# A gated recurrence followed by a highway layer: three pieces of work change engine and the order list is replaced

## The chip, the cores and the metric

The kernel runs on one core of a Trainium2 chip, in one launch. The metric is device microseconds (us) of the whole execution. The core's engines are named as the profile names them: PE (TensorE), with PEld for its weight loads; DVE (VectorE); ACT (ScalarE); POOL (GpSimd); SP, which here only starts DMAs. Each engine works through its own instructions strictly in their order, and waits on semaphores for the others.

## What is computed

```python
B, S, D = 4, 6336, 256
f = lower_bound + (1 - lower_bound) * sigmoid(f_logit)      # B x S x D
h = f[:, t] * h + (1 - f[:, t]) * x[:, t]                   # for every t: y[:, t] = h
y = y.reshape(B * S, D)                                     # 25344 tokens
H = maximum(y @ w_h, 0);  T = sigmoid(y @ w_t + b_t)
out = T * H + (1 - T) * y                                   # float32
```

Inputs are float32: `x` and `f_logit` of 26 MB each, two 256x256 weight matrices, and two vectors. The output has 26 MB.

## The kernel before

The tokens are cut into 25 units: 24 of 1024 tokens of one batch (8 blocks of 128 tokens), and a last one of 8 blocks of 96 tokens that holds the rest of all four batches. A unit goes through a *front* (load, gate, transpose, scan) and a *back* (highway layer, store). At the beginning units are cut finer: unit 0 has fronts 0, 1, 2 of 2, 2 and 4 blocks, units 1 and 2 have two fronts of 4 blocks (3, 4 and 5, 6), and from front 7 on a front is a whole unit. The last unit has fronts 28 and 29 and backs 24 and 25, of 4 blocks. There are 30 fronts and 26 backs; back j uses the scan of front j+4, for j of 3 and more.

Each step has a letter, and the program is written by a list of letters, `PLAN` (L349). The next letter X takes the next piece of kind X. What an engine does, and in which order, is fixed by this list alone. A digit behind A, B, Z, G or O names the PSUM slot that the step writes: slots 0 and 1 for the transposes A and B, slots 0, 1 and 2 for Z, G and O. A slot can be written again when its reader is done. The letters, with the engine and the line:

- L, X (SP, L106): load `f_logit` or `x` of a front, from five buffers each; Q (SP, L125): load one of the two weight matrices. R (SP, L309): store half a back.
- U (ACT, L154): u = sigmoid(-f_logit) for a front. A (PE, L198): transpose u. F (ACT, L205): the decay f, from PSUM.
- P (POOL, L160) and p (DVE, L166): the product bv = u * x of two blocks; a whole unit has four. B (PE, L215): transpose bv. S (DVE, L230): the scan, one for each half of the 256 channels; it reads f and B's PSUM slot.
- W (DVE, L148): scale the weights of one half of the channels; two in all, ahead of the first G.
- G, Z (PE, L245): the two matrix products of a back, four matmuls for each half of the channels. D (DVE, L256): relu with the scaled y, from G's slot. T (ACT, L251): sigmoid, from Z's slot.
- E (DVE, L166) and H (POOL, L160): e = d * t. In a full back, E does the first 512 columns and H the other 512 (`SHARE`).
- O (PE, L296 and L297): the sum with y, transposed back, for half a back. C (ACT, L303) and V (DVE, L303): copy it out of PSUM; V has a share in the last three backs only.

`F4.1` below is the second step F of front 4, `C2.0` the first copy of back 2; steps without a number are all of their kind for that front. DVE's products (E and p) go through `vector_mul`, POOL's (P and H) through `gpsimd_mul`, and the next POOL product in the list after a DVE product is made to wait for it:

```python
def gpsimd_mul(out_, a, b):
    ins = pin(nc.gpsimd.tensor_mul(out_, a, b))
    while port:
        tc.add_manual_dep(ins.ins, port.pop().ins.name, ...reason="shared port")
```

Of the kernel before, what the change touches and what calls it, by code (L numbers as in the profile page):

```python
# [19 lines left out]
def kernel(  # L20
# [19 lines left out]
    P = 128  # L40
    NH = D // P
    NB = 8
# [16 lines left out]
    fronts, backs = [], []  # L59
# [6 lines left out]

    LASTQ = 2

    EARLY = [(0, 0), (2, 0)]

# [40 lines left out]
    def shape(piece):  # L113

        u, j0, j1 = piece
        return units[u][0], j1 - j0
# [34 lines left out]
    def gate(i):  # L151
        np_, nb = shape(fronts[i])
        u = fs[i]["u"] = new("u", [NB, D], FP16)
        pin(nc.scalar.activation(u[:np_, :nb], fs[i]["lt"][:np_, :nb], AF.Sigmoid, scale=-1.0))  # L154
# [13 lines left out]
    def product(i, k, mul):  # L168
        np_, _ = shape(fronts[i])
        if "bv" not in fs[i]:  # L170
            fs[i]["bv"] = new("bv", [NB // 2, D, 2], BF16)
        mul(inner(fs[i]["bv"][:np_, k:k + 1])[:, 0], fs[i]["u"][:np_, 2 * k:2 * k + 2],
            fs[i]["xt"][:np_, 2 * k:2 * k + 2])

    def width(piece):
        np_, nb = shape(piece)
        return np_ * nb
# [81 lines left out]
    SHARE = 512  # L259

    def shared(j):

        return SHARE if width(backs[j]) == NB * P else 0

    def e_cols(j, a, e):
        if "e" not in bs[j]:
# [3 lines left out]
    def e_dve(j):  # L270
        vector_mul(*e_cols(j, 0, width(backs[j]) - shared(j)))

    def e_pool(j):
        gpsimd_mul(*e_cols(j, width(backs[j]) - shared(j), width(backs[j])))
# [37 lines left out]
    def each(pieces, count):  # L312
        return [(i, k) for i, piece in enumerate(pieces) for k in range(count(piece))]

    def halves_of(pieces):
        return each(pieces, lambda p: len(halves(p)))
# [22 lines left out]
        "D": (d_dve, each(backs, lambda p: NH)),  # L339
        "E": (lambda j, _: e_dve(j), each(backs, lambda p: 1)),  # L340
        "H": (lambda j, _: e_pool(j), [(j, 0) for j in range(len(backs)) if shared(j)]),
        "O": (o_pe, groups),
        "C": (lambda j, q: o_copy(j, q, nc.scalar.copy, 0, group(j, q)[2]), [p for p in groups if group(*p)[2]]),
# [3 lines left out]
    }  # L347

    PLAN = (  # L349
        "LLXXLXQQUUA0pFFB1PSLXLXLXLSA0B1UFFpSSWWA0PFFUXLXLB1PSA0PSUFFUPPG0G1Z2B1DDSZ0STTA0B1PPHEFFUPSXXLA0SPF"  # L350
        "FUO1B0O2LLXXA1PSSPCCFFUPG0G1B0PPPDSSDZ2Z0A1A0TTFFEZ2B1Z0A0TTUFG1G2SDDB1HPPPPHPO0O1B0UCCSSZ2A1G0Z1B0E"
        "DTFTPPSPPPA1O2G0O1DHFUCCB1A0G0Z2Z1SFTTA1B0DEPSLLLXXRXRRLXRRRFUPG2O0B1O1A0DPPHCCG2FSDZ0Z1A1B0G2EPSTTF"
        "UPO0O1B1DPPHCCA0G2Z0SFDZ1A1B0EPSTFTUPG2O0A1B0O1DPPHCCG2Z0FSDA0B1Z1EPRRRRXLLSTFTPO2G0B0O1DPUCCESZ0G2A"
        "1Z1TFDB0A1G0PHPSDTFUO2B1O1CCPPPHSA0G0Z2Z1B1DFTEPSA0G0O2TPFDPPHB0O1G0A1UCCFSXLRXRRLRRRLLRXXDZ2Z1B0A1E"
        "PSTTFPO0G2B1A0O1DPPHCUCFSG0Z2Z1B1A0DEPSTTFPG0O2B0O1A1DPPHUCFCSG0Z2DA1B0Z1EPSG0PTFTDPPHB1O2O1G0A0UCCS"
        "Z2B1Z1FTDEPXRXRRRLRSTPA0O0G2O1B1DPPHFCCSA0G0Z2Z1B1DUFTEPSA0G0O2TPFCO1B0A1G2DPPHCSFUDZ0Z1A1B0G2EPSTTF"
        "PLLRRXLXRRXRRDPPHO0O1B0A1CCSFUG0Z2Z1A1B0DTTFEPSPG0O2O1B0A1DPPHCCFUSZ2G0A1B0Z1DEPSTTFPG0O2O1B0A1DPPHC"
        "CFUSG2Z0B1Z1A0RLRRRRXLRXXLLDEPSTFTPG2O0B0O1A1DPPHCUCFSG2Z0B0Z1A1DTTFEPSG2O0B0O1A1PDPPHCUCFSG2Z0B0Z1A"
        "1TFTDEPSPG2O0B1A0G1UCFDPPHSDO2Z0B1A0Z1TFTCPSPG0B0A1EZ1O2FTCUDSG0A1Z1B0RRRRRXRREDHFFO2G0B1TCPSRO1A0O2"
        "PCCFDSERG0G1RDSHZ2Z0B1DFTTSZ2G1O0HTTSDDCO2G1EERDO0CDO2CVRO1RCVZ0RCVTRTEO2O1CVRR"  # L360
    )
    assert all(PLAN.count(k) == len(places) for k, (_, places) in kinds.items())
    todo = {k: iter(places) for k, (_, places) in kinds.items()}
# [31 lines left out]
```

## Time and profile before

| | |
|---|---|
| median of 8 runs | 215.13 us (214.9 to 215.7) |
| the profiled execution | 215.03 us, span 213.2 us |
| busy, share of the span | PE 88%, DVE 92%, ACT 91%, POOL 77% |
| DMA | 78.7 MB, 16 engines busy for 92.7% of the span on the SP queue |
| first scan starts, last copy ends | 8.32 us, 209.72 us |

The span runs from the first instruction to the last in the trace; 1.8 us of the execution's time lie outside it. Rows of groups read: line, engine, operation, output and inputs, shape, count, then busy us and mean ns of one, then the engine's idle time before them and who ended it. Rows of a timeline begin with the start and the duration in us. Instructions of one engine overlap a little in the trace, so that sums are made with the distance from one start to the next where a row gives it.

### The profile page before, as it was taken

To read this page: it belongs to the slowest core of one execution; us is meant where nothing else is said; L and a number is where in the kernel's file an instruction comes from. 1 tells how busy PE (TensorE), PEld (TensorE's weight loads), DVE (VectorE), ACT (ScalarE), POOL (GpSimd) and SP (SyncE) were. 2 spreads that over 40 slices of the span, in tenths; PEclk is the share of its full clock that TensorE was granted. 3 is DMA by queue.
4 is the path that set the end of the run, shared out by engine and by line. 5 is a ranking of instruction groups with operands and counts; after the bars stand their busy time and mean duration, and the time that the engine had idled before them with its cause. 6 is when DMAs were issued, how large, how long until landed. Compare 5 with 4: busy or idle time off the path is not lost.

```text
span 213.2 us, 4575 instructions
## 1 busy us (share of the span) xinstructions
PE 186.7 (88%) x1773; PEld 132.2 (62%) x1800; DVE 196.0 (92%) x156; ACT 194.3 (91%) x194; POOL 164.8 (77%) x134
## 2 busy tenths in 40 slices
PE   0477797889999999999999999999999999999861
PEld 0244764666866666776575777577667667676651
DVE  1599698999999999999999999999999999999971
ACT  4569979999999999999999999999999999996851
POOL 4269987989789988978988897898898889646500
PEclk9999699999999999999999999999999999999997
DMA  4999999999999999999999999999999998547085
GB/s 98 401 421 421 420 417 422 422 414 418 422 416 421 416 417 421 417 420 416 420 421 417 420 415 422 420 397 420 417 410 377 365 277 336 182 184 288 7 350 194
DMA packets 22725, 78.68 MB, mean 369 GB/s; under 512 B 2352, under 2 KB 2864, under 8 KB 22704
## 3 DMA queue, kind: packets, MB, share of 16 engines
q1 hardware_dynamic: 22160, 78.39, 92.7%
q8 instruction: 14, 0.23, 0.4%
q10 hardware_dynamic: 544, 0.00, 0.1%
q14 instruction: 7, 0.06, 0.1%
HBM read 52.43 MB, written 25.95 MB: 368 GB/s over the span
## 4 chain that ended last, share of the span: by engine, by line
PE 39%; ACT 27%; DMA 13%; DVE 12%; issue 5%; SPq 1%; ACTq 0%; DVEq 0%
DMA lt<-in_f_logit_dram 11%; PE gp L245 10%; PE zp L245 9%; ACT f L205 9%; ACT t L251 8%; ACT u L154 7%; DVE y L230 6%; PE op L296 6%; PE op L297 6%; DVE d L256 5%; PE uT L198 5%; PE bT L215 4%; ACT o L303 3%; DMA xt<-in_x_dram 2%; DVE e L166 1%
## 5 line engine op out<-in xcount | busy, mean ns | idle before, releaser
L160 POOL TENSOR_TENSOR bv<-u,xt 128x512 bf16<-128x512 f16 (+1 forms) x98 | 111.9, 1174 | 27.1 <-DVE e L166 9.6
L230 DVE TENSOR_TENSOR_SCAN y<-f,y,bT 128x1024 bf16<-128x1024 f16 (+3 forms) x56 | 106.6, 1917 | 0.8 <-ACT f L205 0.3
L205 ACT ACTIVATE f<-uT,ncc 128x1024 f16<-128x1024 f16 (+3 forms) x60 | 67.5, 1143 | 1.1 <-PE uT L198 1.1
L256 DVE SCALAR_TENSOR_TENSOR d<-y,ncc,gp 128x1024 bf16<-128x1024 bf16 (+1 forms) x52 | 62.5, 1208 | 0.9 <-PE gp L245 0.7
L251 ACT ACTIVATE t<-zp,bt 128x1024 bf16<-128x1024 f32 (+1 forms) x52 | 61.3, 1279 | 1.3 <-PE zp L245 0.9
L245 PEld LDWEIGHTS <-w_sb 128*128 128x128 f16 x400 | 37.8, 98 | 36.8 <-issue 5.0
L154 ACT ACTIVATE u<-lt 128x2048 f16<-128x2048 f32 (+3 forms) x30 | 54.0, 1800 | 6.0 <-DMA lt<-in_f_logit_dram 5.8
L303 ACT COPY o<-op 128x1024 f32<-128x1024 f32 (+2 forms) x50 | 54.2, 1188 | 5.2 <-PE op L297 5.2
L160 POOL TENSOR_TENSOR e<-d,t 128x1024 bf16<-128x1024 bf16 x24 | 51.6, 2150 | 8.7 <-DVE e L166 7.4
L297 PE MATMUL op<-ident_b,e 128*128 128x128 bf16 (+1 forms) x400 | 50.3, 221 | 2.9 <-DVE e L166 1.7
L296 PE MATMUL op<-diag,y 128*128 128x128 f16 (+1 forms) x400 | 50.4, 221 | 0.8 <-ACT t L251 0.7
L245 PE MATMUL gp<-y,w_sb 128*128 128x512 bf16 (+1 forms) x178 | 49.0, 382 | 1.8 <-DVE d L256 0.7
L245 PE MATMUL zp<-y,w_sb 128*128 128x512 bf16 (+1 forms) x195 | 49.1, 376 | 1.3 <-DVE y L230 0.8
L297 PEld LDWEIGHTS <-e 128*128 128x128 bf16 (+1 forms) x400 | 45.0, 115 | 7.1 <-DVE e L166 2.0
L296 PEld LDWEIGHTS <-y 128*128 128x128 bf16 (+1 forms) x400 | 45.1, 115 | 2.3
L215 PE MATMUL bT<-ident_f,bv 128*128 128x128 f32 (+1 forms) x200 | 32.3, 285 | 8.5 <-ACT f L205 2.6
L198 PE MATMUL uT<-ident_h,u 128*128 128x128 f16 (+1 forms) x400 | 31.7, 224 | 7.0 <-ACT u L154 5.4
L198 PEld LDWEIGHTS <-u 128*128 128x128 f16 (+1 forms) x400 | 26.9, 100 | 14.2 <-ACT u L154 5.8
L215 PEld LDWEIGHTS bT<-ident_f,bv 128*128 128x128 f32 (+1 forms) x200 | 23.0, 145 | 16.1 <-POOL bv L160 4.4
L166 DVE TENSOR_TENSOR e<-d,t 128x1024 bf16<-128x1024 bf16 (+1 forms) x26 | 18.5, 714 | 1.1 <-ACT t L251 1.0
L230 DVE TENSOR_TENSOR_SCAN y<-f,bT 128x512 bf16<-128x512 f16 (+2 forms) x8 | 10.5, 1342 | 3.1 <-PE bT L215 3.1
L303 DVE COPY o<-op 128x512 f32<-128x512 f32 (+1 forms) x4 | 2.8, 689 | 1.8 <-PE op L297 1.1
(20 smaller groups left out, 8.8 us busy)
## 6 DMA issues: line engine op xcount, KB each, us to landing
out_dram<-o SPq DMA_DIRECT2D x48, 512.0 KB, 13.5
lt<-in_f_logit_dram SPq DMA_DIRECT2D x21, 1024.0 KB, 15.0
xt<-in_x_dram SPq DMA_DIRECT2D x21, 1024.0 KB, 16.3
lt<-in_f_logit_dram SPq DMA_DIRECT2D x5, 512.0 KB, 7.9
xt<-in_x_dram SPq DMA_DIRECT2D x5, 512.0 KB, 8.6
xt<-in_x_dram SPq DMA_DIRECT2D x2, 384.0 KB, 10.6
lt<-in_f_logit_dram SPq DMA_DIRECT2D x2, 384.0 KB, 16.3
lt<-in_f_logit_dram SPq DMA_DIRECT2D x2, 256.0 KB, 4.0
```

The lines of the kernel that those rows point to most:

```text
L154: pin(nc.scalar.activation(u[:np_, :nb], fs[i]["lt"][:np_, :nb], AF.Sigmoid, scale=-1.0))
L160: ins = pin(nc.gpsimd.tensor_mul(out_, a, b))
L198: pin(nc.tensor.transpose(uT[:, j * np_:(j + 1) * np_], fs[i]["u"][:np_, j, h * P:(h + 1) * P], ident_h[:np_, :np_]))
L205: pin(nc.scalar.activation(f[:, :N].rearrange("p (k q j) -> p k q j", q=np_, j=j), fs[i]["uT", h].rearrange("p (k j q) -> p k q j", q=np_, ...
L215: pin(nc.tensor.transpose(t[:, k // r, k % r], fs[i]["bv"][:np_, k, h * P:(h + 1) * P].rearrange("p d j -> p (d j)").bitcast(FP32), ident_ ...
L230: pin(nc.vector.tensor_tensor_scan(y, fs[i]["f", h][:, c:c + w], fs[i]["bT", h][:, c:c + w], 0.0 if prev is None else prev, op0=ALU.mult, ...
L245: pin(nc.tensor.matmul(p[:, a:e], w_sb[:, k, ki, h * P:(h + 1) * P], y_of(j)[:, ki, a:e], start=ki == 0, stop=ki == NH - 1))
L251: pin(nc.scalar.activation(bs[j]["t"][:, m, :width(backs[j])], bs[j]["zp", m], AF.Sigmoid, bias=bt[:, m:m + 1]))
L256: pin(nc.vector.scalar_tensor_tensor(bs[j]["d"][:, m, :width(backs[j])], y_of(j)[:, m], ncc[:, m:m + 1], bs[j]["gp", m], op0=ALU.mult, op1 ...
L296: pin(nc.tensor.matmul(o, y[:, h, cols], diag[:, h], start=True, stop=False))
L297: pin(nc.tensor.matmul(o, bs[j]["e"][:, h, cols], ident_b, start=False, stop=True))
L303: pin(copy(bs[j]["o", q][:np_, a:e], bs[j]["op", q][:np_, a:e]))
```

## The change

Three things differ.

- `EARLY` is empty. The products of front 0 and the first one of front 2, which DVE made (p), are made by POOL (P).
- `shared` is 512 only from back 3 on. In backs 0, 1 and 2 one E of 1024 columns does all of e, and there is no H.
- `PLAN` is another list throughout, with 823 steps instead of 826.

The change is described as "GpSimd scales the weights instead of VectorE; VectorE alone computes e of the first three full backs; new list with measured durations". In the code W is the same in both kernels: `weights` (L147) issues on `nc.vector`, and the diff doesn't touch it. W's two steps stand at other places of the list.

```diff
-    EARLY = [(0, 0), (2, 0)]
+    EARLY = []
...
     def shared(j):
 
-        return SHARE if width(backs[j]) == NB * P else 0
+        return SHARE if width(backs[j]) == NB * P and j >= 3 else 0
...
     PLAN = (
-        "LLXXLXQQUUA0pFFB1PSLXLXLXLSA0B1UFFpSSWWA0PFFUXLXLB1PSA0PSUFFUPPG0G1Z2B1DDSZ0STTA0B1PPHEFFUPSXXLA0SPF"
-        "FUO1B0O2LLXXA1PSSPCCFFUPG0G1B0PPPDSSDZ2Z0A1A0TTFFEZ2B1Z0A0TTUFG1G2SDDB1HPPPPHPO0O1B0UCCSSZ2A1G0Z1B0E"
-        "DTFTPPSPPPA1O2G0O1DHFUCCB1A0G0Z2Z1SFTTA1B0DEPSLLLXXRXRRLXRRRFUPG2O0B1O1A0DPPHCCG2FSDZ0Z1A1B0G2EPSTTF"
-        "UPO0O1B1DPPHCCA0G2Z0SFDZ1A1B0EPSTFTUPG2O0A1B0O1DPPHCCG2Z0FSDA0B1Z1EPRRRRXLLSTFTPO2G0B0O1DPUCCESZ0G2A"
...
-        "1TFTDEPSPG2O0B1A0G1UCFDPPHSDO2Z0B1A0Z1TFTCPSPG0B0A1EZ1O2FTCUDSG0A1Z1B0RRRRRXRREDHFFO2G0B1TCPSRO1A0O2"
-        "PCCFDSERG0G1RDSHZ2Z0B1DFTTSZ2G1O0HTTSDDCO2G1EERDO0CDO2CVRO1RCVZ0RCVTRTEO2O1CVRR"
+        "XLLLXXLUUA0A1PFFFFUB0PSSA1B0FUFPSSPA0B1XQQLXLXLLXPPWFFUSSWB0A1PFUFPSSPXXLLXLG0Z1B0A1Z2PTFUFTPPG1B1DS"
+        "SDSSUEA0Z0G1G2A1DDPFTFFPPZ0B0A1O1O2PSSTFECCUB1B0Z0G1G2SDSDA1Z1TUFTPPPPPPA1G0B0FLXRLXRXLXLDESA1O1Z2Z0"
+        "UFCTTB1G1A0O2O0SDPPPFCCB0A1Z2G1O0FTUCB1G2PPHPPSDSEDPA0Z1Z0B1O2FTTUCESG1A0G0B1DDHPPPPSO2Z1O0UFTCCB0SA"
...
+        "UFCDEXXLRRRLLXXRRRRRLB1A0Z2G1PSTTFO0DCB1A0Z2G1O0PPHSFUCTDEB0A1G1Z0O2PPSDFTCB1A0G0SFPPHDO1A0B1Z2G0EUC"
+        "TFPPSO1PZ2CDTB0A1Z1G0SFTUHO2A1B0DFG1EPPPPSO0A1CCZ2DFB0Z0O1B1TTCUSESHPPG2A0Z0G1DDRRRRRRRRFFTB0A1O0Z2Z"
+        "1FCFSEHTTG0B1G2O1RSDDCO0SRHCZ2G1STRO0TDDEZ2CTERTG1O0O2DVDCO0CVEVRO1CRO2RCVRR"
     )
```

What moves in the list, in steps:

- The loads begin X0 L0 L1 L2 X1 X2 L3 X3, then Q Q, then L4. Before, they began L0 L1 X0 X1 L2 X2, then Q Q, then L3.
- DVE begins S0 S1 W S2 W S3 D0.0 S4 D0.1 S5 E0 D1.0 D1.1 S6 E1. Before: p S0 p S1 W W S2 D0.0 D0.1 S3 E0 S4 S5 D1.0 S6 D1.1 E1, where E was half as wide.
- PE has the O steps of back 0 behind A7.1, and before had them behind A5.
- At the end, after the last scan, PE has O22.1 Z25 G25 O23.0 O23.1 O24 O25. Before it had O22.1 G25 O23.0 O23.1 O24 Z25 O25.

## The prediction

> **What bounds the kernel now.** I read the page's busy line, then the engines' busy time by stretch, then VectorE's timeline at both ends. These are the stretches; after the stretch and its length come the busy us of PE, PEld, DVE, ACT and POOL, the granted clock, the DMA share and GB/s:
>
> ```profile
> 0.00:20.00 20.00, 10.53 (x59) 6.54 (x60) 12.41 (x20) 12.32 (x18) 10.59 (x20) 1.00 0.88 329
> 20.00:40.00 20.00, 15.94 (x139) 11.60 (x142) 16.85 (x14) 18.62 (x20) 17.21 (x14) 0.91 1.03 420
> 40.00:60.00 20.00, 18.39 (x181) 13.09 (x182) 20.00 (x13) 20.00 (x19) 18.30 (x15) 1.00 1.02 417
> 60.00:120.00 60.00, 57.03 (x564) 40.92 (x571) 59.78 (x41) 60.00 (x56) 53.01 (x41) 1.00 1.03 419
> 120.00:180.00 60.00, 58.34 (x565) 41.19 (x572) 59.51 (x41) 60.00 (x57) 52.57 (x40) 1.00 1.02 392
> 180.00:200.00 20.00, 19.63 (x181) 13.08 (x183) 20.00 (x20) 17.84 (x22) 11.90 (x9) 1.00 0.50 190
> 200.00:213.20 13.20, 6.81 (x100) 5.83 (x98) 7.41 (x13) 5.52 (x9) 1.25 (x1) 0.90 0.59 220
> ```
>
> From 40 to 180 us ACT is never idle, DVE idles 0.7 us and PE 6 of 140 us. There is nothing to gain there and something to lose. DVE idles 10.7 us before 40 us and 5.8 after 200; ACT idles 9.1 and, from 180 on, 9.8. So a change pays in two places: how early both engines have their first work behind them, and how tightly the last backs drain. DMA is full until near 180 us and half idle at the end: loads matter in the first 45 us.
>
> VectorE's timeline at both ends (start, duration, instruction, idle before it and who ended it):
>
> ```profile
> 6.74 0.73 DVE L166 TENSOR_TENSOR bv<-u,xt 128x512 bf16<-128x512 f16 x1 [1.33 <-DMA xt<-in_x_dram]
> 9.91 0.73 DVE L166 TENSOR_TENSOR bv<-u,xt 128x512 bf16<-128x512 f16 x1 [0.33 <-DMA xt<-in_x_dram]
> 26.24 2.33 DVE L230 TENSOR_TENSOR_SCAN y<-f,bT 128x512 bf16<-128x512 f16 x2 [1.84 <-PE bT L215]
> 34.02 1.40 DVE L166 TENSOR_TENSOR e<-d,t 128x1024 bf16<-128x1024 bf16 x1 [0.50 <-ACT t L251]
> ...
> 201.90 1.15 DVE L166 TENSOR_TENSOR e<-d,t 128x1024 bf16<-128x1024 bf16 x2
> 207.34 0.56 DVE L166 TENSOR_TENSOR e<-d,t 128x768 bf16<-128x768 bf16 x1 [0.48 <-ACT t L251]
> 209.03 0.69 DVE L303 COPY o<-op 96x512 f32<-96x512 f32 x1 [1.13 <-PE op L297]
> ```
>
> The 1.84 us at 26.24 is S5: on PE, its transposes B5 stood behind O0.0, and O0.0 waited 1.2 us for H0, which POOL made from 21.04 on in 2.60 us. In the new list O0 stands behind A7.1 and there is no H0. The tail's two waits are one chain: T25 is late, so E25, O25 and the last copy are.
>
> **The engine moves.** Prices by shape:
>
> ```profile
> L160 POOL TENSOR_TENSOR bv<-u,xt 128x512 bf16<-128x512 f16 x94 | 107.3, 1175 | 27.1 <-DVE e L166 9.6 <-DVE bv L166 6.6 <-DMA xt<-in_x_dram 3.8
> L160 POOL TENSOR_TENSOR e<-d,t 128x1024 bf16<-128x1024 bf16 x24 | 51.6, 2150 | 8.7 <-DVE e L166 7.4 <-ACT t L251 1.3
> L166 DVE TENSOR_TENSOR e<-d,t 128x1024 bf16<-128x1024 bf16 x24 | 17.5, 728 | 0.6 <-ACT t L251 0.5
> ```
>
> DVE loses two products of 0.73 us. It made E0, E1, E2 in 0.67, 1.40 and 1.12 us; a full-width E has no row. Two halves in a row took 1.15 us (201.90), twice the row stretched beside POOL would be 2.8; I take 1.2, the nearer row, because in the new list the next POOL step waits for each of these E and none runs beside it. Sum: 3 x 1.2 - 3.19 - 1.46 = -1.05 us of DVE work. POOL: 2 x 1.175 - 3 x 2.15 = -4.1 us, off the path, since it idles some 36 us. The added wait is P7.0 behind E0 (until 28.15 in the walk below). P7.1 to P7.3 queue behind it, until 32.8; B7 waits for them and is done at 33.5. S7.0 has E1 in front of it on DVE until 34.15, so E1 hides the wait by 0.65 us; a later E0 beyond that would delay S7 one for one. "GpSimd scales the weights" isn't in the code; W costs DVE its 2 x 0.70 us as before.
>
> On the price of moving a product to POOL, the row says 1.175 against 0.73 us, a factor of 1.6. The Trainium skill (GPSIMD Engine Reference, 4.1 Engine selection) advises against it: two-input elementwise work is about twice as slow there. By its factor a moved product would cost 1.46 us, 0.3 us more on the way to the first scan.
>
> **The ramp, walked.** Waits that ended on a load date them: L0 4.15, L1 5.84, X0 6.74 for the first three 256 KB; then 1536 KB by 8.53 and 5632 KB by 18.80 us, or 399 KB per us. In the new order X0, L0, L1 take those three times, L2 (1280 KB) 7.9, L3 11.0, the weights (3584 KB) 13.7, before 11.1, and L4 15.0, as before. So U0 starts at 5.84, not 4.15. P0 follows on POOL until 7.7; B0 ends at 8.8 and S0 starts at 8.85 (before 8.32). B1 stands behind A2, which needs U2 (ends 9.9): S1 11.15 (10.53). W0.0 at 13.7, S2 14.4 (13.23), W0.1, S3 17.45 (18.76, because two D stood before it). The A4 step needs S2's slot and starts at 16.85. G0 17.55, D0.0 19.8, S4 21.0, D0.1, S5 24.55 (26.24), E0 26.9, D1 28.15, S6 30.55, E1 32.9, S7.0 34.15 (35.87). From 14.4 on DVE has no idle time in this walk: its input is ready each time, by 0.1 to 3 us. It reaches the same finished work (S9.1, E3, D4.1) at 56.7, where it was 58.00: 1.3 us earlier. ACT, with U8 at 32.95 (L8 lands at 31.7), finishes the same set (F10.0, T4.1, C2.1) at 55.0 instead of 55.84: 0.85 us earlier. ACT is the engine that is never idle afterwards, so the ramp is worth -0.85. Bounds: -1.3 (DVE's lead) to +1.0 (one more wait such as the 1.84 at 26.24).
>
> PE's clock in the ramp: in 20 to 40 us it was 0.91, since 0.107 us lay between O0's matmuls instead of 0.055 from 23.70 to 26.2, after a PE wait of 1.2 us. A second such spell would cost 1.25 us, inside the upper bound above. The Trainium skill (TensorE: Matmul & The Clock Gate, Part 1) has the clock halve only after an idle window of about 3.4 us; no PE gap of the walk is that long, so by the page nothing is charged, while the row shows a shorter gap ahead of one.
>
> **The middle.** Per unit the work is the same. Steps there are U 1.80, F 1.0 x 2, T 1.0 x 2, C 0.9 x 2 on ACT, 7.6 us, and S 2.26 x 2, D 1.18 x 2, E 0.60 on DVE, 7.5. In the new list around units 24 and 25, F24.1 may start 0.65 us earlier to 1.0 us later than steady before either ACT or the scan waits: the PSUM slots leave some slack but not much. I charge the new order 0.65 us, as much idle time again as DVE showed between 40 and 180; bounds 0 and 2.
>
> **The tail.** Measured from S27.0 (186.36 before), DVE has the same work until the last scan, 14.6 us on (200.95). Before, Z25 stood behind O23 and O24 on PE, so T25 ran at 206.26, E25 at 207.34, the last copy 209.03 to 209.72: 23.4 us after S27.0. In the new list Z25 follows the last scan: Z25 0.85, C22.1, T25 until 17.0, D25.0, O23.0 until 17.4, V23.0, D25.1, V23.1 until 19.3, E25 19.85, O25.1 until 20.6, V25.1 20.7 to 21.4. That is -1.95 us, and DVE's idle time after 201.9 (0.29 + 0.20 + 0.20 + 0.48 + 1.13 = 2.3) is the most it can give. F28 comes up to 1.6 us later here (T21.1 stands behind F27.1), covered by S27.1; without that cover it would be 1.6 us back. I take -1.9, bounds -2.3 and 0. From the last copy to the end stay 3.5 us, the last store.
>
> Sum: -0.85 + 0.65 - 1.9 = -2.1, from the profiled 215.03 to 212.9 us. The median of all runs, 215.13, is 0.1 above that execution; 0.2% of this time, 0.43 us, is about what its measurement can tell from no change.
>
> **The rivals.** First, the middle takes the lead back: ACT and DVE are full there for 140 us, and a lead of 1 us only shifts where each waits, while the tail gives half (-0.95). With a charge of 0.9 to 2 in the middle that is 215.03 - 0.85 - 0.95 plus the charge, 214.1 to 215.2; 214.7 at 1.5. For it: DVE's E recurred every 7.46 us at 54 to 76 and 7.62 at 167 to 175, so the faster engine already waits for the other. Against it: the tail's reorder doesn't depend on that.
>
> Second, slower than before: the new list makes ACT wait once in each unit, for a PE step queued behind a slot that isn't free (O18.1 stands ahead of A26 and B25.1, for instance). Place: the 18 units between 45 and 180 us. ACT showed waits of 0.35 (181.44) and 0.58 us (192.82) of this kind when units were no longer regular. At 0.25 us a unit it is 4.5 us against the 2.75 gained, 216.8; it decides from 0.15 us a unit on. For it: PE is 95 to 97% busy there and takes steps in strict order. Against it: the slack above.
>
> Third, more than forecast: no charge in the middle, and DVE's whole lead counts, -1.3 - 1.95: 211.8.
>
> **How the numbers follow.** The forecast has 0.48, the first rival 0.16, the slower one 0.22, the third 0.14. The first lies half within 0.43 us of 215.03. Faster by over 0.2%: 0.48 + 0.14 + 0.08 = 0.70, less 0.03 for the forecast's own upper end: 0.67. Same: 0.08 + 0.02 = 0.10. Slower 0.23. The range goes from 211.0 (the sum of the lower bounds, -3.6, gives 211.4; the runs spread by 0.8 us, so 0.4 to a side) to 216.6, which leaves out over half of the slower rival (0.12) and a few in 100 at the low end. The forecast's own range is 211.4 to 214.8: all terms at their lower bounds, or one of them at its upper.
>
> **What would show it.** Right: S0 near 8.9, W0.0 near 13.7, no DVE idle of over 0.3 us between 15 and 57; D4.1 ends near 56.7; E after 201 without the two waits on T25 and O25, the last copy about 21.5 us after S27.0. Wrong: ACT idle between 60 and 180 us; PE's clock below 0.9 for more than one spell; weights that land after 15 us, which holds S2, A4, F4 and U5 behind W0.0 one for one.

## The result and the profile after

The changed kernel takes 216.29 us (median of 11 runs, 215.5 to 217.05), the old one 215.13 beside it (32 runs). The ratio is 1.005, with an interval of 1.0037 to 1.0063: slower by half a per cent, where 1% faster was forecast. Its profiled execution took 215.5 us with a span of 213.6. It is the fastest of its runs; two more profiles of the same kernel, below, are nearer to the median and show what this one hides.

The stretches of that execution (stretch, its length, busy us of PE, PEld, DVE, ACT and POOL, granted clock, DMA share, GB/s):

```profile
0.00:20.00 20.00, 8.45 (x48) 5.55 (x49) 9.17 (x16) 10.80 (x17) 12.66 (x20) 1.00 0.87 328
20.00:40.00 20.00, 17.32 (x135) 10.77 (x137) 19.71 (x16) 19.43 (x20) 12.50 (x11) 1.00 1.02 420
...
60.00:120.00 60.00, 57.91 (x573) 41.18 (x578) 59.27 (x40) 60.00 (x56) 53.85 (x42) 1.00 1.03 419
120.00:180.00 60.00, 58.43 (x560) 40.68 (x566) 59.87 (x41) 60.00 (x57) 51.07 (x40) 1.00 1.02 399
...
200.00:213.60 13.60, 6.82 (x91) 5.56 (x88) 7.17 (x13) 5.20 (x10) 1.16 (x1) 0.94 0.67 252
```

In the middle ACT is still never idle, so the slower rival of the prediction (a wait of ACT in every unit) did not come. DVE is busy for 3.2 us less in the first 20 us: two products have left it, and its steps D come later. The granted clock of 1.00 in the first row misleads: the trace has no record of the clock before its first change, at 20.9 us, and the matmuls' own durations show half speed until then.

Both sums of the prediction can be read as distances between the same steps. From the start of S9.0 to that of S27.0: 135.8 us before, 136.2 after, +0.4 (forecast +0.65). From S27.0 to the end of the last copy: 23.36 before, 22.21 after, -1.15 (forecast -1.95). From there to the end of the span: 3.5 before, 5.1 after, 5.0 in the two other profiles (forecast: no change). And S9.0 started at 50.53 before, and at 50.11, 51.41 and 51.02 in the three profiles of after: from 0.4 ahead to 0.9 behind, where 0.85 to 1.3 ahead was forecast. So the tail lost 0.3 to 0.5 us instead of giving 1.9, the middle took a little less than was charged, and the ramp went from a gain to a loss in two of the three profiles.

### The profile page after: what moved, and what is told of

It is laid out like the page before. It is cut to its first block, busy times and chain, and to the rows that moved or that the text cites. A ratio compares the mean times of both kernels' runs of the same rounds, so it can differ in the third digit from the quotient of the medians.

```text
span 213.6 us, 4586 instructions
## 1 busy us (share of the span) xinstructions
PE 187.0 (88%) x1775; PEld 131.1 (61%) x1800; DVE 195.0 (91%) x154; ACT 193.7 (91%) x194; POOL 161.5 (76%) x133
## 4 chain that ended last, share of the span: by engine, by line
PE 41%; ACT 35%; issue 11%; DVE 7%; DMA 3%; SPq 0%; ACTq 0%; DVEq 0%
ACT t L251 10%; PE gp L245 9%; PE zp L245 9%; ACT u L154 9%; ACT f L205 8%; ACT o L303 7%; PE uT L198 7%; PE bT L215 5%; PE op L297 5%; PE op L296 5%; DVE y L230 3%; DVE d L256 3%; DMA lt<-in_f_logit_dram 3%; DVE e L166 1%; DVE o L303 1%
## 5 line engine op out<-in xcount | busy, mean ns | idle before, releaser
L160 POOL TENSOR_TENSOR bv<-u,xt 128x512 bf16<-128x512 f16 (+1 forms) x100 | 115.0, 1183 | 29.9 <-DVE e L166 10.6
L205 ACT ACTIVATE f<-uT,ncc 128x1024 f16<-128x1024 f16 (+3 forms) x60 | 65.8, 1109 | 4.3 <-PE uT L198 4.3
L251 ACT ACTIVATE t<-zp,bt 128x1024 bf16<-128x1024 f32 (+1 forms) x52 | 62.6, 1247 | 0.9 <-PE zp L245 0.6
L303 ACT COPY o<-op 128x1024 f32<-128x1024 f32 (+2 forms) x50 | 55.1, 1148 | 4.6 <-DVE o L303 2.6
L154 ACT ACTIVATE u<-lt 128x2048 f16<-128x2048 f32 (+3 forms) x30 | 53.0, 1766 | 3.6 <-DMA lt<-in_f_logit_dram 3.6
L160 POOL TENSOR_TENSOR e<-d,t 128x1024 bf16<-128x1024 bf16 x21 | 44.8, 2136 | 9.3 <-DVE e L166 6.8
L245 PE MATMUL gp<-y,w_sb 128*128 128x512 bf16 (+1 forms) x187 | 50.8, 382 | 1.1 <-ACT t L251 0.3
L296 PE MATMUL op<-diag,y 128*128 128x128 f16 (+1 forms) x400 | 49.6, 219 | 1.8 <-DVE d L256 0.7
L297 PE MATMUL op<-ident_b,e 128*128 128x128 bf16 (+1 forms) x400 | 49.6, 219 | 0.6 <-DVE e L166 0.6
L166 DVE TENSOR_TENSOR e<-d,t 128x1024 bf16<-128x1024 bf16 (+2 forms) x26 | 19.3, 748 | 0.2
```

What stands on the lines that cost most here:

```text
L205: pin(nc.scalar.activation(f[:, :N].rearrange("p (k q j) -> p k q j", q=np_, j=j), fs[i]["uT", h].rearrange("p (k j q) -> p k q j", q=np_, ...
L245: pin(nc.tensor.matmul(p[:, a:e], w_sb[:, k, ki, h * P:(h + 1) * P], y_of(j)[:, ki, a:e], start=ki == 0, stop=ki == NH - 1))
L251: pin(nc.scalar.activation(bs[j]["t"][:, m, :width(backs[j])], bs[j]["zp", m], AF.Sigmoid, bias=bt[:, m:m + 1]))
L296: pin(nc.tensor.matmul(o, y[:, h, cols], diag[:, h], start=True, stop=False))
L297: pin(nc.tensor.matmul(o, bs[j]["e"][:, h, cols], ident_b, start=False, stop=True))
L303: pin(copy(bs[j]["o", q][:np_, a:e], bs[j]["op", q][:np_, a:e]))
```

## The experiments

### Which part costs it: four halves

Each run takes the list of one kernel up to a point and the steps that are left in the order of the other. The ramp ends after 198 steps, near 54 us; the tail begins near 178 us.

```diff
 ramp_new   new list to 54 us, old order from there
 ramp_old   old list to 54 us, new order from there
 tail_new   old list to 178 us, new order from there
 tail_old   new list to 178 us, old order from there
```

> The new list's first 198 steps (to about 54 us), then the old list's order; no DVE products p, no H in backs 0 to 2. Theory 1 (the ramp cost it: ACT reaches the same work 0.45 us later in the new profile, and nothing later gives it back): 215.13 + 0.5 to 1.2, 215.6 to 216.3. Theory 2 (the tail cost it: the last copies come earlier but the last three stores leave together): equal to before within 0.4 us, 214.7 to 215.5. Theory 3 (the middle's order cost it): equal to before too.

> The old list's ramp with its engine assignment (DVE products p, H in backs 0 to 2) up to about 54 us, then the new list's middle and tail. Theory 1 (ramp): back to 215.1 within 0.4 us. Theory 2 (tail) and theory 3 (middle): stays at 216.3, 215.9 to 216.7.

> The old kernel until about 178 us, then the new list's last 126 steps: Z25 ahead of G25, O23 and O24. Theory 1 (ramp) and theory 3 (middle): last copy 1.2 us earlier and the stores take back 0.8 of it, 214.3 to 215.2. Theory 2 (tail): 215.5 to 216.3. My forecast of the tail (-1.9) would be 213.2.

> The new kernel until about 178 us, then the old list's last steps. Theory 1 (ramp): 215.8 to 216.8, as the new kernel or a little later. Theory 2 (tail): back to 215.1 within 0.4. Theory 3 (middle): 216.0 to 216.8.

Measured, with the old kernel at 215.12 beside them: ramp_new 216.68 (ratio 1.0066, 1.004 to 1.0092), ramp_old 216.1 (1.0051, 1.0032 to 1.007), tail_new 215.36 (1.0008, 0.9992 to 1.0025), tail_old 217.67 (1.0108, 1.0085 to 1.0131). The new tail on the old list costs nothing and gives nothing. The new ramp is slow with the old middle and tail behind it. But three of the four say less than was hoped. ramp_old took what the theories of tail and middle had expected: it has the old order up to S9.0, and yet started S9.0 at 51.19 us in its profile where before had 50.53. There the first product began at 7.74 us instead of 6.74, when its x had landed, and the first scan at 9.32 instead of 8.32. In ramp_new and ramp_old the stretch from S9.0 to S27.0 took 136.9 us, longer than in either list (135.8 and 136.2). And tail_old lost 0.9 us more than either list between S26.0 and S27.0, where the two orders meet. So the medians of these three can't be read as the price of one part. What their profiles did show is that the same ramp doesn't take the same time twice: ramp_new and tail_old reach S9.0 at 51.83 and 51.57 us, after at 50.11.

### The same kernel again

```diff
 after_2, after_3: the changed kernel, no edit
```

> The changed kernel itself, profiled a second time, because its first profiled run (215.5 us) lies 0.8 us under its median. In the ten profiles so far the clock of TensorE changes only on a grid of 3.41 us whose phase differs from run to run; it went to full at the end of a 3.41 us stretch in which TensorE was busy for at least 84%, never after one under 82%, and back to half after stretches of 41 to 46%. Theory T-gate (the phase decides when the new ramp gets its full clock): it opens at the end of the first stretch with 84% or more, between 20.5 and 24 us; with 20.5 to 21.5 us S9.0 starts at 50.0 to 50.4 and the run takes 215.5; with 22.5 to 24 us S9.0 starts at 51.3 to 51.9 and the run takes 216.4 to 217. Rival T-W (W beside GpSimd's product decides): the late runs are those in which W0.0 takes 1.75 us instead of 0.75, whatever the clock.

> The changed kernel itself a third time, for the same purpose and with the same expectations as after_2.

They took 216.56 and 216.3 us, and don't separate the two theories: W is slow in both, and the clock is late in both, full for good from 23.69 and 22.47 us. VectorE's timeline in the first profile of after (start, duration, instruction, idle before and who ended it):

```profile
14.12 0.75 DVE L148 SCALAR_TENSOR_TENSOR w_sb<-o,cc 128x512 f16<-128x512 f32 x1 [0.95 <-DMA o<-in_moe_w_h_dram]
15.28 2.45 DVE L230 TENSOR_TENSOR_SCAN y<-f,y,bT 128x512 bf16<-128x512 f16 x2 [0.40 <-PE bT L215]
17.65 0.77 DVE L148 SCALAR_TENSOR_TENSOR w_sb<-o,cc 128x512 f16<-128x512 f32 x1
18.34 2.32 DVE L230 TENSOR_TENSOR_SCAN y<-f,bT 128x512 bf16<-128x512 f16 x2
```

and in after_2:

```profile
14.38 1.61 DVE L148 SCALAR_TENSOR_TENSOR w_sb<-o,cc 128x512 f16<-128x512 f32 x1 [1.11 <-DMA o<-in_moe_w_h_dram]
15.91 2.44 DVE L230 TENSOR_TENSOR_SCAN y<-f,y,bT 128x512 bf16<-128x512 f16 x2
18.27 1.50 DVE L148 SCALAR_TENSOR_TENSOR w_sb<-o,cc 128x512 f16<-128x512 f32 x1
19.70 2.32 DVE L230 TENSOR_TENSOR_SCAN y<-f,bT 128x512 bf16<-128x512 f16 x2
```

W, the same instruction on the same data, takes 0.75 us in one and 1.61 in the other, and the scan S3.0 behind the second W starts 1.36 us later (after_3: 1.73 and 1.36 us, S3.0 at 19.20). POOL's products P3 (first row) and P4 (second) beside it, in after:

```profile
13.06 2.83 POOL L160 TENSOR_TENSOR bv<-u,xt 128x512 bf16<-128x512 f16 x2 [0.45 <-ACT u L154]
16.71 2.73 POOL L160 TENSOR_TENSOR bv<-u,xt 128x512 bf16<-128x512 f16 x2 [0.81 <-ACT u L154]
```

and in after_2:

```profile
13.16 2.29 POOL L160 TENSOR_TENSOR bv<-u,xt 128x512 bf16<-128x512 f16 x2 [0.29 <-ACT u L154]
16.95 2.28 POOL L160 TENSOR_TENSOR bv<-u,xt 128x512 bf16<-128x512 f16 x2 [1.50 <-PE bT L215]
```

Two products take 2.29 us where W is slow and 2.73 to 2.83 where W is fast: one of the two engines waits. Which one, the order of their starts decides: in after W starts at 14.12 and 17.65, ahead of the second product of each pair (14.18 and 17.83), and in after_2 at 14.38 and 18.27, behind it (14.28 and 18.07). Over the seven profiles in which they meet (the three of after, ramp_new, tail_old and, below, the two of after_warm) the first to start went through for 12 of 14 W; in the other two W started 0.02 and 0.04 us ahead and waited all the same. The Trainium skill (GPSIMD Engine Reference, 8. Key points) says that GpSimd shares its SBUF interfaces with VectorE and that instructions of VectorE with two inputs from SBUF, or in what it calls a 2-port mode, contend with it; W has two (the weights and `ndiag`), and these rows give the price. Before, both W together took 1.39 us (11.82 on), while POOL stood idle from 11.94 to 13.82 us.

The other suspect is PE's clock (TensorE's). Over the traces of all 20 profiles it changes only on a grid of 3.41 us, whose phase differs from run to run. These stretches, cut along that grid, show it in before; PE is the first of the five busy columns and the clock stands behind them (the first row's 1.00 is again the missing record, it ran at half):

```profile
12.70:16.11 3.41, 2.87 (x15) 1.47 (x14) 2.96 (x3) 2.05 (x3) 2.29 (x2) 1.00 1.02 419
...
19.53:22.94 3.41, 1.53 (x20) 1.20 (x17) 3.12 (x4) 3.41 (x5) 3.41 (x3) 1.00 1.03 422
22.94:26.35 3.41, 2.65 (x21) 2.59 (x22) 1.57 (x3) 3.41 (x4) 2.97 (x3) 0.50 1.03 420
```

and in after, where both 1.00 are the missing record:

```profile
14.07:17.49 3.42, 2.24 (x11) 1.40 (x8) 2.96 (x3) 2.21 (x3) 2.61 (x3) 1.00 1.02 419
17.49:20.90 3.41, 3.02 (x13) 1.68 (x15) 3.41 (x5) 1.97 (x3) 2.16 (x3) 1.00 1.03 420
```

A stretch with 2.87 or 3.02 us of work is followed by full clock, one with 2.24 is not, and after 1.53 us of work full clock goes back to half. Over all the traces, in the first 40 us, it opened after stretches that were 73 to 100% busy, stayed at half after up to 81%, closed after 31 to 51% (by PE's busy column, which counts the modelled ends of matmuls), and stayed full after 54% and more. The texts above put the lower bound for opening at 84%, which later traces corrected. The Trainium skill (TensorE: Matmul & The Clock Gate, Part 1) describes such a window of about 3.4 us that runs freely and doesn't reset with the kernel; the grid agrees. The page closes the clock after an idle window, and here half-busy ones were enough.

What the moment of the change is worth, one pair of traces shows almost alone. after and tail_old have the same ramp, and in both W takes 0.75 and 0.77 us; the clock is full from 20.90 us in after and from 23.93 in tail_old. S9.0 starts at 50.11 and 51.57 (first row after, second tail_old):

```profile
50.11 2.33 DVE L230 TENSOR_TENSOR_SCAN y<-f,y,bT 128x1024 bf16<-128x1024 f16 x1
51.57 2.33 DVE L230 TENSOR_TENSOR_SCAN y<-f,y,bT 128x1024 bf16<-128x1024 f16 x1
```

Of these 1.46 us, 0.15 were there at S0.0 and S3.0 already. In after, G0.0 (four matmuls) is the last full step at half speed, and half of Z0.0 already runs at full; in tail_old these were PE's steps:

```profile
18.83 1.91 PE L245 MATMUL gp<-y,w_sb 128*128 128x512 bf16 x4
20.54 0.63 PE L245 MATMUL zp<-y,w_sb 128*128 128x512 bf16 x1
21.39 1.06 PE L245 MATMUL zp<-y,w_sb 128*128 128x512 bf16 x2 [0.22 <-issue]
22.24 1.06 PE L215 MATMUL bT<-ident_f,bv 128*128 128x128 f32 x4
23.10 1.01 PE L198 MATMUL uT<-ident_h,u 128*128 128x128 f16 x8
23.94 1.03 PE L245 MATMUL zp<-y,w_sb 128*128 128x512 bf16 x4
```

Four matmuls of 512 columns take 1.91 us at half clock and 1.03 at full, and B4 and A5, on which S4 and F5 wait, stand behind them on PE.

### W by other instructions, and W apart from the products

```diff
 after_w_split
-    scalar_tensor_tensor(w_sb[:, :, h], w_raw[:, :, h], cc, ndiag[:, :, h], mult, add)
+    tensor_scalar(w_sb[:, 1, h], w_raw[:, 1, h], cc, None, mult)             # 256 columns
+    tensor_scalar(w_sb[:, 0, h, other], w_raw[:, 0, h, other], cc, None, mult)  # 128
+    scalar_tensor_tensor(w_sb[:, 0, h, own], w_raw[:, 0, h, own], cc, ndiag[:, 0, h, own], mult, add)
 after_w_port: steps P3.0 P3.1 W0.0 ... W0.1 listed as P3.0 W0.0 W0.1 P3.1, and
-    pin(nc.vector.scalar_tensor_tensor(w_sb[:, :, h], ...))
+    port.append(pin(nc.vector.scalar_tensor_tensor(w_sb[:, :, h], ...)))
```

> The changed kernel with W made of other instructions: 384 of its 512 columns by tensor_scalar (one operand from SBUF and a scalar per partition) and only the 128 columns that hold the diagonal by scalar_tensor_tensor with ndiag; what is computed stays the same. T-W (VectorE's operation with two operands in SBUF and GpSimd's product beside it slow one another: W 0.75 and the product 1.72 us, or W 1.75 and the product 1.17): W0 takes 0.6 to 0.9 us in three pieces, the products beside it stay at 1.17 to 1.3 us, S2.0 and S3.0 start 0.2 to 0.6 us earlier, the median falls from 216.3 to 215.7 - 216.0 and the upper runs of 217 go. T-gate: the median stays within 0.2 us of 216.3.

after_w_split: 216.7 us, ratio 1.0063 (1.0039 to 1.0088), no better. The two tensor_scalar took 2.03 us together in W0 while P3 kept its 2.34: they stand back for GpSimd as the two-input form does, though only one tensor comes from SBUF. The one of 128 columns took 1.19 us beside the product in W0, and 0.27 in W1, where the product had just ended. So leaving out the second operand is no cure.

> The changed kernel with W0.0 and W0.1 listed together ahead of the product P3.1, and that product made to wait for them, as the kernel already makes GpSimd's products wait for VectorE's. Theory T-W (W beside GpSimd's products is the main price of the new ramp: of three profiles of the changed kernel the one with W at 0.75 and 0.77 us is the fast one, the two with 1.61 and 1.50, 1.73 and 1.36 us start S3.0 0.9 to 1.3 us later): both W take 0.70 to 0.75 us, end at about 15.6 us, S2.0 starts at 15.5, S3.0 at 17.9 to 18.2 (18.34, 19.69, 19.21), P3.1 runs 15.6 to 16.8; the median falls from 216.3 to 215.1 - 215.6. What is left of the scatter is the clock. Rival T-gate (the moment of TensorE's full clock alone sets the ramp): median 216.1 to 216.4 with W at 0.7 us.

after_w_port: 216.08 us (215.72 to 216.22), ratio 1.0047 (1.0031 to 1.0062). VectorE's timeline:

```profile
14.18 1.41 DVE L148 SCALAR_TENSOR_TENSOR w_sb<-o,cc 128x512 f16<-128x512 f32 x2 [0.94 <-DMA o<-in_moe_w_h_dram]
15.51 2.44 DVE L230 TENSOR_TENSOR_SCAN y<-f,y,bT 128x512 bf16<-128x512 f16 x2
17.90 2.33 DVE L230 TENSOR_TENSOR_SCAN y<-f,bT 128x512 bf16<-128x512 f16 x2
20.86 1.28 DVE L256 SCALAR_TENSOR_TENSOR d<-y,ncc,gp 128x1024 bf16<-128x1024 bf16 x1 [0.62 <-PE gp L245]
22.79 2.45 DVE L230 TENSOR_TENSOR_SCAN y<-f,y,bT 128x512 bf16<-128x512 f16 x2 [0.65 <-PE bT L215]
```

W is at 0.7 us again, and S3.0 starts at 17.90, 1.8 us ahead of after_2, where the text expected it. But at D0.0 and S4.0 VectorE waits for PE, which has half clock until 21.9 us here. S9.0 starts at 50.70, 0.7 us ahead of after_2 and 0.3 ahead of after_3, but the clock was full earlier too. Beside one another, these are all profiles of the new ramp without extra matmuls, in the order of the clock:

| run | W0.0 and W0.1, us | full clock for good from | S9.0 starts |
|---|---|---|---|
| after | 0.75, 0.77 | 20.90 | 50.11 |
| after_w_port | 0.75, 0.74 | 21.85 | 50.70 |
| after_w_port_cv (below) | 0.75, 0.74 | 22.25 | 50.99 |
| after_3 | 1.73, 1.36 | 22.47 | 51.02 |
| after_w_split (three instructions each) | 2.29, 1.59 | 23.49 | 51.59 |
| ramp_new | 1.74, 1.36 | 23.61 | 51.83 |
| after_2 (also full from 16.86 to 20.28) | 1.61, 1.50 | 23.69 | 51.41 |
| tail_old | 0.75, 0.77 | 23.93 | 51.57 |

S9.0 follows the clock, with slow W and with fast W. So W's price is real at S3.0, but what of it reaches S9.0 is not shown: at an equal clock, between nothing (after_3) and some 0.4 us (ramp_new), an estimate from the distances in this table. The median fell by 0.2 us, which the two intervals don't separate. The six runs lie within 0.5 us, but the twelve of after_w_port_cv, with the same ramp, scatter by 1.5 as those of after do.

### The clock kept full

All these kernels have extra work: TensorE multiplies the identity with itself, and nobody reads it. A step Y of n such matmuls stands ahead of the steps named.

```diff
+    def keep(n, slot):
+        spare = psum(slot, [NB * P], "spare", FP32)
+        for _ in range(n):
+            pin(nc.tensor.matmul(spare[:, :P], ident_b, ident_b, start=True, stop=True))
 after_warm, after_w_port_warm: 40 ahead of A0.0, 8 A1.0, 4 B0.0, 14 A2.0, 18 A3.0, 6 B3.0, 12 A4.0
 before_warm:  28 ahead of A0.0, 28 B0.0, 14 B1.0, 8 B2.0, 6 A3.0, 14 B4.0 (slot 2)
 after_w_port_keep_cv: 40 A0.0, 12 A1.0, 6 B0.0, 15 A2.0, 18 A3.0, 44 B3.0, 4 A4.0
 before_keep_cv: as before_warm, but 22 ahead of B4.0 in slot 1, and 20 ahead of O0.0
```

> The new list with extra work that nobody reads: TensorE multiplies the identity with itself (128x128, bf16) 40 times before its first transpose and 4 to 18 times in its gaps up to the first gp matmul at about 18.7 us, so that it is never long without work. Theory T-PE (the new ramp's price is TensorE's half clock, which ends at 20.9 us in the profiled run of after and at 23.6 to 23.9 us in two grafts with the same ramp): the 512-column matmuls take 379 ns from the first one on instead of 634, S9.0 starts at 49.0 to 49.8 us (after 50.11, the grafts 51.6 to 51.8), the median falls from 216.3 to 214.8 - 215.5, and the runs lie closer together than the 1.5 us of after. Rival T-load (the ramp is set by the loads, by GpSimd's products and by W; TensorE has slack): clock full early as well, but S9.0 no earlier than 50.0 us and the median 216.0 to 216.4. If the extra matmuls get in the way: slower than 216.5.

> after_warm a second time: its first profiled run (215.36 us, S9.0 at 49.47) was the fastest of its seven, the others took 216.6 to 217.5 us with full clock from before 11 us by their mean clocks of 0.981 to 0.991. T-gate alone: clock full by 11 us, S9.0 at 49.3 to 49.7 and 215.3 us again. Rival T-W: W0.0 at 1.75 us, S2.0 about 1 us later than 14.94, S9.0 at 50.4 to 51 and 216.5 to 217 us. If the difference lies after the last copy: S9.0 at 49.5 and the span still 215.

> The old kernel with the same kind of extra identity matmuls that nobody reads (28 before the first transpose, 6 to 28 in the gaps up to 21 us). T-PE: full clock at the first gp matmul (14.5 us) instead of from 16.1 us, and no half-clock spell at 22.9 to 26.35 us, which stretched 28 small matmuls of back 0 and four transposes from about 0.055 to 0.107 us each; S9.0 at 49.6 to 50.2 us (before 50.54), median 214.2 to 214.8. Rival T-load: 215.0 to 215.3, S9.0 at 50.4 to 50.6.

after_warm: 216.83 us, ratio 1.0068 (1.0043 to 1.0093): no gain, and the first reading was that the clock had no part in it. before_warm: 215.03, 0.9993 (0.9975 to 1.0011), no difference. The profiled run of after_warm, the fastest of its seven, did what T-PE expected: full clock from 10.80 us without a break, and S9.0 at 49.47. The second profile of after_warm (216.07 us) shows one thing that went wrong: the clock was full from 6.95 us, but closed again from 17.19 to 20.60, just over the first products of back 0. In the stretch ahead of that PE had 1.73 of 3.41 us of work, since the products P3 and P4, held up by W and a late load, left it idle, and 6 matmuls don't fill that. It reached S9.0 at 49.97, 0.5 us later, and took 5.9 us from its last copy to the end, where after took 5.0 to 5.1. In before_warm the group ahead of B4.0 waited for its PSUM slot and delayed B4.0 by 0.6 us (21.65 against 21.05 in tail_new_cv). The six runs of after_warm at 216.6 to 217.5 us were not profiled, so their median is explained in part only.

> after_w_port with the extra identity matmuls of after_warm (nobody reads them). T-W with the clock as second term (a late clock costs up to 1.4 us: S9.0 at 51.57 with full clock from 23.9 us against 50.11 from 20.9, W equal): W at 0.7 us and the clock full by 11 us, S9.0 at 49.0 to 49.6, median 214.6 to 215.2, and the runs within 0.8 us of one another. If the clock is worth nothing once W is apart: equal to after_w_port within 0.2 us. If neither is the cause: 216.3 or more, as after_warm with 216.83.

after_w_port_warm: 216.54 us, 1.0057 (1.0037 to 1.0077), again no gain. Its stretches on the grid:

```profile
14.46:17.88 3.42, 1.07 (x12) 0.73 (x10) 3.13 (x4) 1.75 (x3) 1.79 (x3) 1.00 1.02 419
17.88:21.29 3.41, 3.19 (x25) 2.59 (x24) 2.87 (x3) 1.10 (x2) 1.78 (x2) 0.50 1.03 416
```

With P3.1 held behind W, PE idles even more, and the clock closes at 17.88 us. The next version fills that place.

> after_w_port_warm_cv with the extra identity matmuls laid out anew (nobody reads them): 44 instead of 6 ahead of the transposes of product P3, where TensorE stood idle in the first version while GpSimd waited for W (a 3.41 us stretch with 31 to 45% work closed the clock again just before the first gp matmul, at 17.0 to 20.4 us), and 4 instead of 12 ahead of A4.0, which they delayed by 1 us at half clock. Theory T-gate as second term: full clock from 7 to 11 us on without a break, first gp matmuls 379 ns, S4.0 at 21.6 to 22.1 (after_w_port 22.79), S9.0 at 49.4 to 50.0, median 214.4 to 215.0. If the clock is worth nothing beside W: equal to after_w_port_cv, 215.2 to 215.6.

213.94 us (213.70 to 214.44), ratio 0.9937 (0.9916 to 0.9958). The same stretches:

```profile
13.88:17.29 3.41, 3.00 (x50) 2.79 (x48) 2.77 (x4) 1.86 (x3) 1.69 (x2) 1.00 1.02 411
17.29:20.70 3.41, 3.02 (x23) 1.78 (x25) 3.41 (x4) 1.91 (x4) 2.28 (x2) 1.00 1.03 420
```

and PE's timeline from the second stretch on:

```profile
19.01 0.81 PE L245 MATMUL gp<-y,w_sb 128*128 128x512 bf16 x3
19.66 1.03 PE L245 MATMUL zp<-y,w_sb 128*128 128x512 bf16 x4
20.67 0.63 PE L215 MATMUL bT<-ident_f,bv 128*128 128x128 f32 x4
```

The clock is full from 7.05 us on, B4 is ready at 21.3 instead of 23.0 us in after_w_port_cv (215.39 us, below), which differs only by the extra matmuls. S9.0 (first row after_w_port_cv, second this run):

```profile
50.99 2.33 DVE L230 TENSOR_TENSOR_SCAN y<-f,y,bT 128x1024 bf16<-128x1024 f16 x1
49.52 2.33 DVE L230 TENSOR_TENSOR_SCAN y<-f,y,bT 128x1024 bf16<-128x1024 f16 x1
```

That is 1.47 us at S9.0, though S3.0 started 0.14 later here (18.21 against 18.07). The medians lie 1.45 us apart, and by the ratios to the old kernel beside each it is 0.8%, or 1.7. It is about the price of the pair of traces above, although the clock's moment moves by 15.2 us here and by 3.0 there: in both it is the steps from G0 to A5, at 18.8 to 24 us in tail_old, that run at half or at full speed.

### The tail

```diff
 tail_new_cv: last steps of tail_new
-  C23.1 V23.1 E25.0 V24.0 R23.0 O25.0 C24.0 R23.1
+  C23.1 V23.1 C24.0 E25.0 V24.0 R23.0 O25.0 R23.1
```

> tail_new with one letter moved: ScalarE's copy of back 24 (C24.0) is listed ahead of E25.0 and V24.0 instead of after O25.0, so that it no longer waits 1.8 us for VectorE's copy into the same tile. Theory T-order (the new tail gives its gain back because E25 on VectorE stands before V24, and C24 behind V24): C24.0 starts at about 205.8 instead of 207.65 us, the store of back 24 leaves about 0.6 us earlier, the last copy ends 0.3 to 0.5 us earlier, and the median falls from 215.36 to 214.8 - 215.0. Rival T-store (the last microseconds are the transfers: all stores land at 212.0 in before and after although the last copy is 1.2 us earlier in after): the copies move, the end does not, 215.2 to 215.4.

214.74 us (214.03 to 215.25), ratio 0.9971 (0.9957 to 0.9985), where tail_new had 1.0008. ACT and DVE fill two column ranges of the same tile, and they do it one after the other, in the order of the list. The tail of after on ACT:

```profile
204.44 1.07 ACT L303 COPY o<-op 128x512 f32<-128x512 f32 x2 [0.75 <-DVE o L303]
207.33 1.07 ACT L303 COPY o<-op 96x512 f32<-96x512 f32 x2 [1.82 <-DVE o L303]
```

and on DVE:

```profile
205.55 0.69 DVE L303 COPY o<-op 128x512 f32<-128x512 f32 x1 [0.62 <-ACT o L303]
206.15 0.55 DVE L166 TENSOR_TENSOR e<-d,t 128x768 bf16<-128x768 bf16 x1
206.62 0.68 DVE L303 COPY o<-op 96x512 f32<-96x512 f32 x1
207.83 0.69 DVE L303 COPY o<-op 96x512 f32<-96x512 f32 x1 [0.53 <-PE op L297]
```

ACT waits 1.82 us ahead of C24.0: PE is done with O24 at 206.2, but V24.0 comes first, and stands behind E25 on DVE. So back 24, the first rows of the last stores, is complete at 207.9 us, and its store leaves together with the two of back 25: SP issues them at 207.94, 208.42 and 208.86, in before at 206.88, 209.19 and 209.74. In the last microseconds the engines then move less than the 418 GB/s they moved shortly before:

```profile
206.00:207.00 1.00, 0.43 (x8) 0.28 (x6) 1.00 (x3) 0.00 (x0) 0.00 (x0) 1.00 1.01 418
...
208.00:209.00 1.00, 0.00 (x0) 0.00 (x0) 0.52 (x1) 0.40 (x1) 0.00 (x0) 1.00 0.60 227
209.00:210.00 1.00, 0.00 (x0) 0.00 (x0) 0.00 (x0) 0.00 (x0) 0.00 (x0) 1.00 1.00 260
210.00:211.00 1.00, 0.00 (x0) 0.00 (x0) 0.00 (x0) 0.00 (x0) 0.00 (x0) 1.00 0.94 307
```

In tail_new_cv, on ACT:

```profile
206.39 0.58 ACT L303 COPY o<-op 96x512 f32<-96x512 f32 x1 [0.65 <-PE op L297]
207.61 0.58 ACT L303 COPY o<-op 96x512 f32<-96x512 f32 x1 [0.64 <-PE op L297]
```

C24.0 is 1.26 us earlier than in tail_new (207.65), the waits for DVE are gone, and the store of back 24 leaves at 207.72 us instead of 208.26, as expected. One part of the expectation missed: the last copy still ends 22.2 us after S27.0. What became shorter is the rest: from the last copy to the end 4.2 us instead of 4.5 in the two profiles, while the medians lie 0.6 apart. So the profiles show half of the gain, and that time itself varies, from 4.2 to 5.9 us over all profiles with the new tail.

> after_w_port with C24.0 listed ahead of E25.0 and V24.0 as in tail_new_cv (which was 0.6 us under tail_new). If both readings hold: 0.5 to 0.7 us under after_w_port, 214.5 to 215.0, under both kernels. If T-gate holds: 215.5 to 215.8.

after_w_port_cv: 215.39 us, ratio 1.0017 (1.0002 to 1.0032), 0.7 us under after_w_port: the tail's edit is worth about the same in the new list.

### Everything together

> before_warm and tail_new_cv together: the old ramp and middle with the extra identity matmuls, and the new tail with C24.0 first. T-PE and T-order: the two gains add, 213.7 to 214.4 us, under both kernels. With T-load and T-store: 215.0 to 215.4.

> All three together: W apart, the extra identity matmuls in the ramp, C24.0 first in the tail. If the three terms add: 214.0 to 214.6 us, under both kernels and under tail_new_cv (214.74). If the clock's term is nothing: 214.5 to 215.0. If the ramp's price is elsewhere: 215.7 or more.

> before_warm_cv with the extra identity matmuls of the gap at 19.5 to 21 us in the PSUM slot that is free from 18.8 us on (in before_warm they waited for ScalarE's T0.1 until 20.9 and delayed B4.0 by 0.6 and A5.0 by 1.3 us), and 20 more while TensorE waits 1.2 us for GpSimd's part of e ahead of O0.0. T-gate: no half-clock spell between 7 us and the end, S5.0 at 25.0 to 25.3 and S9.0 at 50.2 to 50.5 in every run, median 214.2 to 214.7, under tail_new_cv (214.74), with no runs over 215.3. If the spells cost nothing: 214.7 to 214.9 like tail_new_cv. If the extra matmuls are in the way again: over 215.3.

before_warm_cv: 215.95 us, 1.004 (1.002 to 1.006). In its profile the clock closes for two grid steps, 22.76 to 29.59 us, after a stretch with 46% work; over its 12 runs the time goes with the mean granted clock, from 215.0 us at 0.998 to 217.1 at 0.973 (correlation -0.90). after_w_port_warm_cv: 216.44, 1.0057 (1.0038 to 1.0077), with the clock closed from 17.0 to 20.4 us as in after_w_port_warm. before_keep_cv: 214.52, 0.997 (0.9955 to 0.9984), the same ratio as tail_new_cv. It kept the clock full, but its 20 extra matmuls ahead of O0.0 stood in front of real work (O0.0 went on at 25.2 instead of 23.7 us), and its weights came 0.7 us later, so it doesn't tell what the clock is worth in the old list. The profiles of before and tail_new_cv do in part. They have the same ramp; before has a spell of half clock from 22.94 to 26.35, and tail_new_cv has full clock from 15.56 on without one. S5.0 and E1 in tail_new_cv:

```profile
25.18 2.33 DVE L230 TENSOR_TENSOR_SCAN y<-f,bT 128x512 bf16<-128x512 f16 x2 [0.96 <-PE bT L215]
34.11 1.39 DVE L166 TENSOR_TENSOR e<-d,t 128x1024 bf16<-128x1024 bf16 x1 [1.81 <-ACT t L251]
```

S5.0 is 1.06 us ahead of before (26.24), but E1 then waits 1.81 us for ACT instead of 0.50, and S9.0 starts at 50.63 where before has 50.53. So in the old ramp one such spell costs nothing further on; two in a row, in before_warm_cv, go with S9.0 at 51.81.

The best version is after_w_port_keep_cv: the new list with W apart, the clock kept full and C24.0 first, 0.6% under the old kernel and, by the two ratios, 1.1% under the changed one.

## Why the prediction was wrong

**The ramp (forecast -0.85, bounds -1.3 to +1.0).** The step that failed is "PE's clock in the ramp", which charged nothing. It took the 23.7 us spell of before as the only place, though before itself ran at half clock until 16.11 us (its matmuls of 512 columns took 634 ns from 14.51 on), which the 1.00 of the first row hides. It set a rule about gaps of 3.4 us against the row, and left the row in the upper bound. The row showed half clock after a 1.2 us gap, and the runs show that what counts is the work in a whole 3.41 us stretch. The new ramp gives PE 8.45 us of work in its first 20 instead of 10.53, and its clock opens at 20.9 to 23.9 us instead of 15.6 to 19.6, or opens and closes again (after_2: full from 16.86, half from 20.28 to 23.69). In the old ramp it closes again too (before, tail_new), but there the spell costs nothing further on. In the new ramp the clock's moment is worth about 1.5 us, measured twice: 1.46 at S9.0 between 20.90 and 23.93, and 1.47 between 7.05 and 22.25.

A second step, "W costs DVE its 2 x 0.70 us as before", took a price from a place where POOL stood still. In the new list P3.1 and P4.1 run beside W; W took 1.36 to 1.73 us in after_2 and after_3, and S3.0 came up to 1.36 us later. That it reaches S9.0 is not shown.

With W apart and the clock full, in after_w_port_keep_cv, DVE's walk held: S7.0 starts at 34.42 (walked: 34.15) and S9.0 1.01 us ahead of before (forecast: 0.85 to 1.3). ACT's walk, whose 0.85 the sum took, did not: F10.0, T4.1 and C2.1 are finished there at 57.0 instead of 55.0. One step, F10.1 with 1.0 us, is done in addition by then; the other 1.0 stays open. Two landings were taken too early as well: S0 began at 9.0 to 9.4 us instead of 8.85, with L1 at 6.8 to 7.15 instead of 6.74, and S2.0 at 15.3 to 15.9 instead of 14.4, partly since the weights landed at 13.9 to 14.4 instead of 13.7.

**The engine moves.** E0 took 1.20 us as taken, E1 1.23 and E2 1.43; the products on POOL 1.16 to 1.17 where nothing ran beside them. Within 0.2 us these prices held. So did the place of E0 in front of P7.0.

**The middle (forecast +0.65).** +0.4 in all three profiles of after: nearly right, and the two rivals that put 0.9 to 4.5 us there were wrong. Nor does the middle take a lead back: after_w_port_keep_cv, 1.0 us ahead at S9.0, has the same +0.4.

**The tail (forecast -1.9).** Two terms were mis-sized. The last copy came 1.15 us closer to S27.0 instead of 1.95, since the walk let C and V of one half back run side by side: V23.1 waited 0.62 us for C23.1, and E25 started where the walk has it end. The rest is O25, which took 1.13 us from the end of E25 to V25.1 (206.70 to 207.83), as in before, where the walk has 0.85. And "from the last copy to the end stay 3.5 us, the last store" became 5.0 to 5.1: it was a walk of engines, and the end is one of stores, three of which now leave within 1 us. tail_new, with a ratio of 1.0008, has the two terms together behind the old list. That tail_new_cv takes 0.6 us off with one letter shows that the order of the copies was part of it; how the remaining 4.2 to 5.1 us split into transfers and what follows them was not tried, so the cause of the longer end is shown in part only.

Summed for after_3 and after_2: +0.5 and +0.9 in the ramp, +0.35 in the middle, +0.35 in the tail, +1.2 and +1.6, which are the differences of their spans to that of before (214.4 and 214.8 against 213.2). The medians differ by 1.16, or 0.5%. Against the sum of -2.1 the tail is off by 2.2 us, the ramp by 1.3 and 1.7, the middle by 0.3 the other way. None of the rivals had this mechanism: the slower one was right in its sign alone, and its 216.8 lies near the measured 216.29 by luck, since ACT didn't wait in the middle.

## What to carry to other kernels

Price an operation by the neighbours it will have, not only by its shape: a step that ran beside an idle engine before is not the same step beside that engine's stream. When an order is thinned out at the start, look at how much TensorE has to do in each 3.4 us, and read its clock from the durations of the matmuls; 139 useless matmuls in the right holes paid here 1.45 us, and some 100 in the wrong ones lost up to 1.2. Ask also whether the next wait takes an early step's lead away, as E1's did in the old ramp. And follow a tail to the stores: the copy that completes a store matters, not the last copy alone.

## What the runs showed of the hardware

- VectorE's scalar_tensor_tensor with two inputs from SBUF (128x512 float32) takes 0.70 to 0.75 us alone, and 1.24 to 1.74 beside GpSimd's tensor_tensor, or leaves that at 1.6 to 1.7 instead of 1.17 us. The one that starts later waits (12 of 14 cases; in the other two the starts lay 0.02 and 0.04 us apart). A tensor_scalar of 128 float32 columns is held up the same way: 1.19 us instead of 0.27.
- TensorE's clock goes back to half after a 3.41 us stretch in which it had work for as much as 1.73 us (51%); the longest gap in the seven that did this was 1.0 to 1.9 us. It stayed full after stretches of 54% and more.
- The trace has no record of the clock before its first change; until then the profile shows full clock while 512-column matmuls take 634 ns instead of 379.
- The same program reached the same step 1.3 us apart in three runs (50.11, 51.02 and 51.41 us). The phase of the clock's grid and the winner between W and the product differ from run to run, and so do the loads: the same list had its first x 1.0 us later in ramp_old than in before.
